# Third buffer for both split feed-forward weights, with their loads and splits written one group earlier (adaLN + S4D + ReLU feed-forward, one core)

## The chip, the cores and the metric

One core of one Trainium2 chip. The metric is the device time of one launch in microseconds (us). The kernel before takes 1416.15 us, the median of 3 runs (1416.11 to 1416.56).

## What is computed

One transformer-like block over 2048 tokens of width 576, in float32: a modulation from `c`, a layer norm, an S4D long convolution with a skip, a gated residual, a second layer norm, a ReLU feed-forward of 576 -> 4608 -> 576, and a second gated residual.

```python
mod = (_silu(c) @ w_mod).reshape(c.shape[0], 6, 1, -1)
sa, ca, ga, sb, cb, gb = (mod[:, i] for i in range(6))
h = _layernorm(x) * (1 + ca) + sa
x = x + ga * _A_ref(h, ...)      # S4D: K = 2 Re(C P); y = irfft(rfft(u) * rfft(K)); y + u * D_skip
h = _layernorm(x) * (1 + cb) + sb
x = x + gb * _B_ref(h, w1, w2)   # max(h @ w1, 0) @ w2, w1 576 x 4608, w2 4608 x 576
```

## The kernel before

Every large matmul is done in three products: each operand is split into a high part (type fp32r) and a low part, the rest, and high x high, high x low and low x high are added up in PSUM.

**Stages.** The tokens are taken in 4 blocks of 512. A prologue (to 229 us) makes what the first block needs: the convolution kernel's first part, the convolution of block 0, the second norm, and the normed, transposed activations as `xh`, `xl` and `xs` (high, low, and the packed fifth slice). Then the feed-forward runs in 144 groups, 36 per block; one group takes 128 of the 4608 hidden columns. Beside the groups of a block run generators for the rest: in block 0 the rest of the convolution kernel (VectorE rotations into `W1r`, TensorE products `kps`) and the convolution of block 1; in block 1 the output of block 0 and the convolution of block 2; in block 2 the output of block 1 and the convolution of block 3; in block 3 the output of block 2. `step()` draws from them at a rate per block; it is called four times per group, within `first` and `second` and behind each.

**One group.** `load_r1(g)` (L1230) and `load_r2(g)` (L1234) bring the raw weights: `r1`, 320 KB, 128 hidden columns of the first matrix, and `r2`, 288 KB, as many rows of the second; both are issued by SyncE (SP) into tiles with two buffers. `split1(g)` makes `w1`: ScalarE (ACT) copies the high part (L1246) and VectorE (DVE) subtracts for the low part (L1249). `split2(g)` does the same for `w2` (ACT L1256, DVE L1259 and L1260). The DVE parts exist in block 0 only: there the low parts are stored to DRAM (`L1d`, `L2d`; the list `late`, L1348, on SP's queue), and from group 36 on they are loaded back instead, `w<-L1d` in `low1` (L1239) and `w<-L2d` in `split2` (L1263), also on SP's queue. `w1` and `w2` tiles have two buffers each. `first(g)` is 14 matmuls (L1273) of `xs`, `xh`, `xl` with `w1` into `hps`; ACT makes `hh` = relu (L1278) and DVE `hl`, its low part (L1279). `second(g)` is 14 matmuls (L1299) of `hh`, `hl` with `w2` into five accumulators `acc`.

**Order.** What is written through `Kept` keeps the order of the program on its engine, and shows with the line L47 in the profile. Everything else is put in order, engine by engine, by a scheduler, so the order written in `ffn` is its input and not its outcome. In the loop, group g writes: the load of `r1` two groups ahead and of `r2` one group ahead, the stores that are due, `split2(g)`, `split1(g+1)`, `first(g)`, `low1(g+2)`, a step, `second(g-1)`. Every engine runs its own list in order, so an instruction that waits holds back all behind it; SP's list holds the loads of `r1`, `r2`, both low parts and the stores.

**Names in the convolution.** `Z` are evacuated transforms, `K`, `U`, `Ua` spectra of kernel and input, `T` and `Y` the complex products (DVE, L994 to L1000), `V` and `W` what the inverse transform `ps_i` (TensorE, L1021) reads, `x` the residual stream that DVE updates from `ps_i`. `Ua` is loaded back from DRAM (`Ud`) by GpSimd (POOL).

Of the kernel before, what the change touches and what calls it, by code (L numbers as in the profile page):

```python
# [11 lines left out]
F32R = mybir.dt.float32r  # L12
# [6 lines left out]
P = 128  # L19
# [30 lines left out]
class KGen:  # L50
# [10 lines left out]
    def v(self, out, a, b, op):  # L61
        self.tc.keep_in_program_order(self.nc.vector.tensor_tensor(out, a, b, op=op))
# [471 lines left out]
class Body:  # L534
# [198 lines left out]
    def main(self, ctx, kg, hooks):  # L733
# [31 lines left out]
        with ExitStack() as c:  # L765
            self.cps = self.pool(c, "cps0", space=PSUM)
            self.tps = self.pool(c, "tps", space=PSUM)
            self.cv = self.pool(c, "cv0", side="right")
            self.cvl = self.pool(c, "cvl", side="right")
            self.nps = 4  # L770
            mods, ffn = self.mod_late(), self.ffn(gens)
            self.vec = Kept(tc, nc.vector)
            for w in self.conv(0):
                if w == "mod":
                    next(mods, None)
                elif w in ("weights", "split"):
                    next(ffn)
                elif w == "rows":
                    hooks[w]()
                elif w in hooks:  # L780
                    for _ in hooks[w]:
                        pass
            self.vec = nc.vector
# [437 lines left out]
    def ffn(self, gens):  # L1221

        nc, I, ff = self.nc, self.I, self.ff
        n = NB * NF
        r1, r2, w1, w2 = {}, {}, {}, {}
        late = []

        def load_r1(g):
            r1[g] = ff.tile([P, 5, P], F32, tag="r1", bufs=2, name="r1")
            nc.sync.dma_start(out=r1[g], in_=I["w1"][g % NF])  # L1230

        def load_r2(g):
            r2[g] = ff.tile([P, D], F32, tag="r2", bufs=2, name="r2")
            nc.sync.dma_start(out=r2[g], in_=I["w2"][(g % NF) * P : (g % NF) * P + P, :])  # L1234

        def low1(g):
            w = w1[g] = ff.tile([P, 2, 5, P], F32R, tag="w1", bufs=2, name="w1")
            if g >= NF:
                nc.sync.dma_start(  # L1239
                    out=w[:, 1].rearrange("p k c -> p (k c)").bitcast(F32), in_=self.L1d[g % NF]  # L1240
                )

        def split1(g):

            w, r = w1[g], r1.pop(g)
            nc.scalar.activation(w[:, 0], r, AF.Copy)  # L1246
            vec = Kept(self.tc, nc.vector) if g < 3 else nc.vector
            if g < NF:
                vec.tensor_tensor(w[:, 1], r, w[:, 0], op=ALU.subtract)  # L1249
                late.append((self.L1d[g], w[:, 1].rearrange("p k c -> p (k c)")))  # L1250

        def split2(g):

            w = w2[g] = ff.tile([P, 1152], F32R, tag="w2", bufs=2, name="w2")
            r = r2.pop(g)
            nc.scalar.activation(w[:, 0:D], r, AF.Copy)  # L1256
            if g < NF:
                v = (Kept(self.tc, nc.vector) if g < 2 else nc.vector).tensor_tensor
                v(w[:, D:640], r[:, 512:D], w[:, 512:D], op=ALU.subtract)  # L1259
                v(w[:, 640:], r[:, :512], w[:, :512], op=ALU.subtract)  # L1260
                late.append((self.L2d[g], w[:, D:]))
            else:
                nc.sync.dma_start(out=w[:, D:].bitcast(F32), in_=self.L2d[g % NF])  # L1263

        def first(g):
            xh, xl, xs = self.xT[g // NF]
            w = w1.pop(g)
            ps = self.fps.tile([P, 512], F32, tag="hps", bufs=2, name="hps")
            ops = [(w[:, 0, 4], xs), (w[:, 1, 4], xs)]
            for k in range(4):  # L1270
                ops += [(w[:, 0, k], xh[:, k]), (w[:, 0, k], xl[:, k]), (w[:, 1, k], xh[:, k])]
            for i, (a, x) in enumerate(ops):
                nc.tensor.matmul(ps, a, x, start=(i == 0), stop=(i == 13))  # L1273
                if i == 6:
                    step(g)
            hh = ff.tile([P, 512], F32R, tag="hh", bufs=2, name="hh")
            hl = ff.tile([P, 512], F32R, tag="hl", bufs=2, name="hl")
            nc.scalar.activation(hh, ps, AF.Relu)  # L1278
            nc.vector.scalar_tensor_tensor(hl, ps, 0.0, hh, op0=ALU.max, op1=ALU.subtract)  # L1279
            return hh, hl  # L1280

        def second(g, hh, hl):
            f = g % NF
            if f == 0:
                self.acc = [
                    self.fps.tile([P, 512], F32, tag=f"acc{i}", name=f"acc{i}_{g}")
                    for i in range(5)
                ]
            acc, w = self.acc, w2.pop(g)
            tail = [(4, w[:, 512:640], hh), (4, w[:, 512:640], hl)]  # L1290
            ops = []
            for i in range(4):
                tk = slice(i * P, (i + 1) * P)
                ops += [(i, hh[:, tk], w[:, 0:512]), (i, hh[:, tk], w[:, 640:]), (i, hl[:, tk], w[:, 0:512])]
            ops = tail + ops if f == NF - 1 else ops + tail
            seen = [0] * 5
            for j, (i, a, x) in enumerate(ops):
                seen[i] += 1
                nc.tensor.matmul(  # L1299
                    acc[i], a, x,  # L1300
                    start=(f == 0 and seen[i] == 1),
                    stop=(f == NF - 1 and seen[i] == (3 if i < 4 else 2)),
                )
                if j == 6:
                    step(g)

        done, recent = [0.0], []

        def step(g):

            at[0] += 1
            target = self.rate(g // NF) * (at[0] % 144 or 144)
            gen = gens[g // NF]
            v = pe = 0.0
            room = (9.0, 7.0, 7.0, 7.0)[g // NF] - sum(recent[-3:])
            recent.append(0.0)
            while done[0] < target and v < min(room, 2.7) and pe < 2:
                w = next(gen, 0)
                if gen.gi_frame is None or w == -1:
                    return  # L1320
                if w is None:
                    pe += 1
                    done[0] += 0.7
                else:
                    v += w
                    recent[-1] = v
                    done[0] += w

        at = [0]
        load_r1(0)  # L1330
        load_r1(1)
        load_r2(0)
        yield
        low1(0)
        low1(1)
        split1(0)
        split2(0)
        split1(1)
        yield
        prev = None  # L1340
        for g in range(n + 1):
            if g < n:
                if g + 2 < n:
                    load_r1(g + 2)
                if g + 1 < n:
                    load_r2(g + 1)
                for dst, src in late:
                    nc.sync.dma_start(out=dst, in_=src.bitcast(F32))  # L1348
                late.clear()
                if g:  # L1350
                    split2(g)
                    if g + 1 < n:
                        split1(g + 1)
                new = (g, *first(g))
                if g + 2 < n:
                    low1(g + 2)
                step(g)
            if prev is not None:
                second(*prev)
                if prev[0] % NF == NF - 1:  # L1360
                    self.evacuate(prev[0] // NF)
            if g < n:
                prev = new
                step(g)
                if g % NF == NF - 1:
                    for _ in gens[g // NF]:
                        pass
                    done[0] = 0.0
# [126 lines left out]
```

## Time and profile before

| what | value |
|---|---|
| median of 3 runs | 1416.15 us |
| the profiled execution's own device time | 1418.65 us |
| its span on the core | 1416.8 us |
| TensorE (PE) busy | 1263.9 us (89%), 10720 matmuls |
| VectorE (DVE) busy | 891.7 us (63%) |
| ScalarE (ACT) busy | 495.4 us (35%) |
| GpSimd (POOL) busy | 180.1 us (13%) |
| DMA | 348.21 MB, mean 246 GB/s |

The mean granted TensorE clock of that execution is 0.938. By stage, each row a stretch of the span:

| stretch, us | what runs | PE busy, us | DVE busy, us | DMA share |
|---|---|---|---|---|
| 0 to 229 | prologue | 140.76 | 189.00 | 0.70 |
| 229 to 300 | feed-forward of block 0, kernel rotations | 65.75 | 64.03 | 0.71 |
| 300 to 400 | the same | 94.24 | 77.93 | 0.72 |
| 400 to 500 | the same, transforms of block 1 | 91.86 | 66.66 | 0.77 |
| 500 to 570 | end of block 0 | 57.51 | 51.37 | 0.71 |
| 570 to 700 | last of block 0, start of block 1 | 112.82 | 102.73 | 0.71 |
| 700 to 800 | block 1 | 100.00 | 50.88 | 0.76 |
| 800 to 890 | end of block 1 | 83.92 | 76.94 | 0.85 |
| 890 to 1000 | into block 2 | 110.00 | 54.75 | 0.65 |
| 1000 to 1100 | block 2 | 98.06 | 93.75 | 0.91 |
| 1100 to 1407 | end of block 2, block 3 | 307.00 | 58.77 | 0.63 |

How to read it: busy shares say little by themselves. A stretch in which PE is busy throughout can only be shortened by fewer matmuls or a higher clock; in the others, what ended PE's idle time (the releaser, written `<-` behind a row) says what set the pace.

### The profile page before, as it was taken

What the parts mean: (1) busy time and instruction counts of PE and PEld (TensorE: products, weight loads), DVE (VectorE), ACT (ScalarE), POOL (GpSimd) and SP (SyncE); (2) the same over time, 40 slices, a digit from 0 to 9 for tenths busy, and PEclk for the clock granted to TensorE, in tenths of its full rate; (3) what the DMA queues carried; (4) which work ended last, traced back from release to release, by engine and by line L of the source; (5) the groups of instructions that cost most, each with busy time, mean ns of one, the idle gap of its engine ahead of it and who ended that gap; (6) DMA issues with size and microseconds to landing.
All of it is one profiled execution on the core that took longest, in us unless ns stands there. A gap on an engine that the chain in (4) does not pass through costs nothing.

```text
span 1416.8 us, 26161 instructions
## 1 busy us (share of the span) xinstructions
PE 1263.9 (89%) x10720; PEld 996.0 (70%) x10720; DVE 891.7 (63%) x1324; ACT 495.4 (35%) x863; POOL 180.1 (13%) x277
## 2 busy tenths in 40 slices
PE   4665687999988987788999998999999999999997
PEld 2444555777867765566777786777887878888886
DVE  5899967999574776958835779463889432101102
ACT  4688323122221431161224322633322253323321
POOL 0667521000110100011010110010000000000000
PEclk9577777999999998899999999999999999999999
DMA  8658865867696767569777988585989657666662
GB/s 255 246 193 313 315 224 181 288 214 256 239 374 228 256 223 280 167 253 346 282 243 252 339 295 293 159 282 152 375 294 350 201 153 228 194 201 195 195 198 98
DMA packets 120845, 348.21 MB, mean 246 GB/s; under 512 B 23949, under 2 KB 24245, under 8 KB 109717
## 3 DMA queue, kind: packets, MB, share of 16 engines
q1 hardware_dynamic: 102260, 222.09, 47.9%
q0 software_dynamic: 17952, 123.08, 22.9%
q8 instruction: 84, 1.38, 0.4%
q10 hardware_dynamic: 512, 1.38, 0.3%
q14 instruction: 37, 0.30, 0.1%
HBM read 262.73 MB, written 83.76 MB: 245 GB/s over the span
## 4 chain that ended last, share of the span: by engine, by line
PE 66%; DVE 8%; DMA 7%; issue 2%; ACT 1%; POOL 0%; SPq 0%; POOLq 0%; ACTq 0%; DVEq 0%
PE hps L1273 28%; PE acc L1299 28%; PE kps L490 4%; PE ps_f L815 3%; DMA w<-L2d 2%; DMA L1d<-w 2%; DMA w<-L1d 2%; PE ps_i L1021 1%; DVE T L459 1%; DVE Y L1000 1%; DVE W1r L461 1%; DMA Ud<-U 1%; DVE T L998 1%; DVE W1r L465 0%; DVE w L1249 0%
## 5 line engine op out<-in xcount | busy, mean ns | idle before, releaser
L1273 PE MATMUL hps<-xh,w 128*128 128x512 f32 x1152 | 396.4, 404 | 0.0
L1299 PE MATMUL acc<-w,hh 128*128 128x512 f32 x1152 | 370.5, 403 | 6.6 <-DMA w<-L2d 6.2
L1279 DVE SCALAR_TENSOR_TENSOR hl<-hps,hh 128x512 fp32r<-128x512 f32 x144 | 99.1, 688 | 326.5 <-ACT hh L1278 326.2
L1299 PEld LDWEIGHTS acc<-w,hh 128*128 128x128 f32 x1152 | 217.3, 190 | 56.8 <-DMA w<-L2d 7.5
L1273 PEld LDWEIGHTS hps<-xh,w 128*128 128x128 f32 x1152 | 220.7, 192 | 48.6 <-ACT xh L1116 0.2
L1299 PE MATMUL acc<-w,hl 128*128 128x512 f32 x576 | 228.3, 409 | 13.2 <-DVE hl L1279 13.2
L1273 PE MATMUL hps<-xl,w 128*128 128x512 f32 x576 | 235.1, 408 | 1.6 <-DVE xl L47 1.6
L1278 ACT ACTIVATE hh<-hps 128x512 fp32r<-128x512 f32 x144 | 86.0, 597 | 366.0 <-PE hps L1273 364.2
L1256 ACT ACTIVATE w<-r 128x576 fp32r<-128x576 f32 x144 | 98.8, 686 | 251.4 <-issue 175.4
L1299 PEld LDWEIGHTS acc<-w,hl 128*128 128x128 f32 x576 | 109.7, 191 | 37.5 <-DVE hl L1279 14.1
L1273 PEld LDWEIGHTS hps<-xl,w 128*128 128x128 f32 x576 | 110.9, 193 | 26.6 <-DVE xl L47 2.7
L1273 PE MATMUL hps<-xs,w 128*128 128x512 f32 x288 | 101.7, 422 | 17.8 <-DMA w<-L1d 7.2
L1246 ACT ACTIVATE w<-r 128x640 fp32r<-128x640 f32 x144 | 105.4, 732 | 34.6 <-DMA L1d<-w 34.5
L490 PEld LDWEIGHTS kps<-W1r,W2r 128*32 128x32 f32 x3456 | 68.1, 146 | 39.8 <-issue 28.2
L490 PE MATMUL kps<-W1r,W2r 128*32 128x48 f32 (+2 forms) x3456 | 78.3, 238 | 14.9 <-issue 11.5
L71 PE MATMUL kps<-W,W 128*32 128x16 f32 x2304 | 45.1, 218 | 44.2 <-POOL W L68 29.0
L71 PEld LDWEIGHTS kps<-W,W 128*32 128x32 f32 x2304 | 40.5, 150 | 55.7 <-POOL W L68 31.4
L1000 DVE TENSOR_TENSOR Y<-Y,T 128x1152 f32<-128x1152 f32 x60 | 79.4, 1350 | 0.0
L1273 PEld LDWEIGHTS hps<-xs,w 128*128 128x128 f32 x288 | 55.0, 194 | 33.4 <-DMA w<-L1d 8.9
L816 ACT ACTIVATE Z<-ps_f 128x288 f32<-128x288 f32 x120 | 48.8, 408 | 68.8 <-PE ps_f L815 67.6
L1409 POOL DMA_DIRECT2D out_dram<-x x16 | 8.7, 546 | 462.8 <-DVE x L1401 460.4
L1299 PE MATMUL acc<-hh,w 128*128 128x512 f32 x144 | 57.4, 398 | 2.5 <-DVE w L1259 1.3
(234 smaller groups left out, 1590.1 us busy)
## 6 DMA issues: line engine op xcount, KB each, us to landing
r<-in_w_dram SPq DMA_DIRECT2D x144, 320.0 KB
r<-in_w_dram SPq DMA_DIRECT2D x144, 288.0 KB, 3.2
w<-L1d SPq DMA_DIRECT2D x108, 320.0 KB, 3.7
w<-L2d SPq DMA_DIRECT2D x108, 288.0 KB
W2r<-W2d POOLq DMA_DIRECT2D x18, 1536.0 KB, 8.8
W2d<-W SPq DMA_DIRECT2D x12, 1536.0 KB, 8.6
Ua<-Ud POOLq DMA_DIRECT2D x15, 1152.0 KB, 10.2
W<-W1d POOLq DMA_DIRECT2D x18, 768.0 KB, 9.4
```

Source lines behind the costliest of these rows:

```text
L71: self.tc.keep_in_program_order(self.nc.tensor.matmul(*args, **kw))
L459: v(T.rearrange(flat), X.rearrange(flat), zi, op=ALU.mult)
L490: nc.tensor.matmul(ps[32 * dd : 32 * dd + 32, q, :], W2[:, r, :, ch], W1[:, :, r, ch], start=(r == 0), stop=(r == 1),)
L815: nc.tensor.matmul(o, fc[:, n2, c, :], src(n2), start=True, stop=True)
L816: ev = nc.scalar.activation(Z[:, n2, c], ps[:, :PC], AF.Copy)
L1000: v(y, y, T, op=op or ALU.add)
L1246: nc.scalar.activation(w[:, 0], r, AF.Copy)
L1256: nc.scalar.activation(w[:, 0:D], r, AF.Copy)
L1273: nc.tensor.matmul(ps, a, x, start=(i == 0), stop=(i == 13))
L1278: nc.scalar.activation(hh, ps, AF.Relu)
L1279: nc.vector.scalar_tensor_tensor(hl, ps, 0.0, hh, op0=ALU.max, op1=ALU.subtract)
L1299: nc.tensor.matmul(acc[i], a, x, start=(f == 0 and seen[i] == 1), stop=(f == NF - 1 and seen[i] == (3 if i < 4 else 2)),)
```

## The change

`w1` and `w2` get a third buffer; `r1` and `r2` keep two. In the loop the loads of the raw weights are written one group earlier (`r1` three groups ahead, `r2` two), `split2` works for group g+1 and `split1` for group g+2 and both stand behind `first(g)`, and `low1` (with the reload of the low part) works for group g+3. Ahead of the loop two more raw loads are issued and a third `w1` tile is asked for. The DVE part of a split keeps its program order (`Kept`) for groups 0 and 1 of `w1` (before: 0 to 2) and for group 0 of `w2` (before: 0 and 1).

```diff
         def low1(g):
-            w = w1[g] = ff.tile([P, 2, 5, P], F32R, tag="w1", bufs=2, name="w1")
+            w = w1[g] = ff.tile([P, 2, 5, P], F32R, tag="w1", bufs=3, name="w1")
...
-            vec = Kept(self.tc, nc.vector) if g < 3 else nc.vector
+            vec = Kept(self.tc, nc.vector) if g < 2 else nc.vector
...
-            w = w2[g] = ff.tile([P, 1152], F32R, tag="w2", bufs=2, name="w2")
+            w = w2[g] = ff.tile([P, 1152], F32R, tag="w2", bufs=3, name="w2")
...
-                v = (Kept(self.tc, nc.vector) if g < 2 else nc.vector).tensor_tensor
+                v = (Kept(self.tc, nc.vector) if g < 1 else nc.vector).tensor_tensor
...
-        low1(0)
-        low1(1)
+        for g in range(3):
+            low1(g)
         split1(0)
         split2(0)
         split1(1)
         yield
+        load_r2(1)
+        load_r1(2)
         prev = None
         for g in range(n + 1):
             if g < n:
+                if g + 3 < n:
+                    load_r1(g + 3)
                 if g + 2 < n:
-                    load_r1(g + 2)
-                if g + 1 < n:
-                    load_r2(g + 1)
+                    load_r2(g + 2)
                 for dst, src in late:
                     nc.sync.dma_start(out=dst, in_=src.bitcast(F32))
                 late.clear()
-                if g:
-                    split2(g)
-                    if g + 1 < n:
-                        split1(g + 1)
                 new = (g, *first(g))
+                if g + 1 < n:
+                    split2(g + 1)
                 if g + 2 < n:
-                    low1(g + 2)
+                    split1(g + 2)
+                if g + 3 < n:
+                    low1(g + 3)
                 step(g)
```

What it moves on the engines. First, DVE in the prologue, at the first complex product of the convolution of block 0 and the second product that follows it; `w_2977` is `w2` of group 1 and `w_3018` that of group 2, `r_2938` and `r_2944` their raw weights.

```order
 L47 TENSOR_TENSOR Y_0_2710<-Y_0_2710,T 128x4x288
 L47 TENSOR_TENSOR T<-K_0_2659,U_0_2633 128x1152
+L1259 TENSOR_TENSOR w_2977<-r_2938,w_2977 128x64
 L47 TENSOR_TENSOR Y_0_2710<-Y_0_2710,T 128x4x288
+L1260 TENSOR_TENSOR w_2977<-r_2938,w_2977 128x512
 L47 TENSOR_TENSOR V_0_2719<-Y_0_2710 128x576 x4
 L47 TENSOR_TENSOR K_1_2724<-Z 128x576 x2
```

The low part of `w2` of group 1 has moved from behind the start of the feed-forward to a place between the last two steps of that product, and the low part of group 2 stands in the second product in the same way.

Second, DVE in the second norm of block 0, and ACT at the same place; `w_2839` is `w1` of group 2, `r_2940` its raw weights.

```order
 L47 TENSOR_TENSOR x_0_280<-ps_i,x_0_280 128x4x72
 L47 BN_STATS st_2819<-x_0_280 128x6 x2
+L1249 TENSOR_TENSOR w_2839<-r_2940,w_2839 128x640
 L47 BN_AGGR mv_288<-st_2819 128x2
 L47 RECIPROCAL mv_288<-mv_288 128x1
```

```order
 L857 ACTIVATE Z<-ps_f 128x288 x3
+L1256 ACTIVATE w_3018<-r_2944 128x576
 L714 ACTIVATE row_gb<-mps_gb 128x128
 L716 ACTIVATE row_gb<-mps_gb 32x64 x2
+L1246 ACTIVATE w_2839<-r_2940 128x640
 L47 ACTIVATE mv_288<-mv_288,eps 128x1 x2
```

Both halves of that split now stand inside the norm, ACT's copy ahead of the square root `mv` and DVE's subtraction ahead of the aggregation; they stood behind the start of the feed-forward.

Third, PE behind `second(0)` at the start of the feed-forward, before (`w_2972` is `w1` of group 2 there, `w_2985` is `w2` of group 1, `w_3011` `w1` of group 3):

```order
L1299 MATMUL acc_0_3017<-hl,w_2841 128x512
L1273 MATMUL hps<-xs_2816,w_2972 128x512
L1299 MATMUL acc_0_3013<-w_2985,hh 128x512
L1299 MATMUL acc_0_3014<-w_2985,hh 128x512
L1299 MATMUL acc_0_3015<-w_2985,hh 128x512
L1299 MATMUL acc_0_3016<-w_2985,hh 128x512
L1273 MATMUL hps<-xs_2816,w_3011 128x512
L1299 MATMUL acc_0_3017<-hh,w_2985 128x512
```

and now (`w_2839` is `w1` of group 2, `w_2977` is `w2` of group 1):

```order
L1299 MATMUL acc_0_3030<-hl,w_2842 128x512
L1273 MATMUL hps<-xs_2816,w_2839 128x512 x2
L1273 MATMUL hps<-xh_2814,w_2839 128x512
L1273 MATMUL hps<-xl_2815,w_2839 128x512
L1273 MATMUL hps<-xh_2814,w_2839 128x512 x2
L1273 MATMUL hps<-xl_2815,w_2839 128x512
```

Single matmuls of `first` and `second` of different groups alternated there, each waiting for its part; now all of `first(2)` stands ahead of `second(1)`.

## The prediction

> **What bounds the kernel now.** I read the chain of waits first, its shares by engine and by line.
>
> ```profile
> PE 66%; DVE 8%; DMA 7%; issue 2%; ACT 1%; POOL 0%; SPq 0%; POOLq 0%; ACTq 0%; DVEq 0%
> PE hps L1273 28%; PE acc L1299 28%; PE kps L490 4%; PE ps_f L815 3%; DMA w<-L2d 2%; DMA L1d<-w 2%; DMA w<-L1d 2%; PE ps_i L1021 1%; DVE T L459 1%; DVE Y L1000 1%; DVE W1r L461 1%; DMA Ud<-U 1%; DVE T L998 1%; DVE W1r L465 0%; DVE w L1249 0%
> ```
>
> Two thirds are matmuls, which the change leaves alone. But 2% each go to the reloads of the low parts (`w<-L1d`, `w<-L2d`) and the stores (`L1d<-w`): the transfers around the two tiles that get a third buffer. In order of time, the longest such pieces (start, duration) are:
>
> ```profile
> 295.27 11.28 DMA L1d<-w
> ...
> 554.10 15.81 DMA L1d<-w
> 629.00 17.10 DMA w<-L2d
> 800.19 10.13 DMA w<-L1d
> 846.38 15.61 DMA w<-L2d
> 1056.04 12.60 DMA w<-L1d
> ```
>
> The groups by line say what engines lost to them (last column: idle time before, and its releasers).
>
> ```profile
> L1299 PE MATMUL acc<-w,hh 128*128 128x512 f32 x1152 | 370.5, 403 | 6.6 <-DMA w<-L2d 6.2 <-ACT hh L1278 0.2
> L1299 PE MATMUL acc<-w,hl 128*128 128x512 f32 x576 | 228.3, 409 | 13.2 <-DVE hl L1279 13.2
> L1273 PE MATMUL hps<-xs,w 128*128 128x512 f32 x288 | 101.7, 422 | 17.8 <-DMA w<-L1d 7.2 <-ACT w L1246 3.9 <-DVE hl L1279 2.3
> L1246 ACT ACTIVATE w<-r 128x640 fp32r<-128x640 f32 x144 | 105.4, 732 | 34.6 <-DMA L1d<-w 34.5
> ```
>
> PE waited 7.2 + 6.2 = 13.4 us for reloads, 3.9 for a copy. ACT waited 34.5 us before its copies into `w1`, because the store that reads the tile's previous contents had not landed: a wait for a buffer. Single rows of PE's timeline place the waits:
>
> ```profile
> 248.26 0.47 PE L1273 MATMUL hps<-xs,w 128*128 128x512 f32 x1 [2.30 <-DVE hl L1279]
> 249.97 0.50 PE L1299 MATMUL acc<-hh,w 128*128 128x512 f32 x1 [1.24 <-DVE w L47]
> ...
> 308.34 1.29 PE L490 MATMUL kps<-W1r,W2r 128*32 128x48 f32 x48 [3.25 <-ACT ker L500]
> ...
> 565.38 0.80 PE L1273 MATMUL hps<-xs,w 128*128 128x512 f32 x1 [3.90 <-ACT w L1246]
> ...
> 588.23 2.07 PE L1299 MATMUL acc<-w,hl 128*128 128x512 f32 x4 [8.04 <-DVE hl L1279]
> ...
> 639.78 0.80 PE L1273 MATMUL hps<-xs,w 128*128 128x512 f32 x1 [2.76 <-DMA w<-L1d]
> ...
> 862.03 0.80 PE L1299 MATMUL acc<-w,hh 128*128 128x512 f32 x1 [3.59 <-DMA w<-L2d]
> ...
> 1068.68 0.50 PE L1273 MATMUL hps<-xs,w 128*128 128x512 f32 x1 [1.94 <-DMA w<-L1d]
> ```
>
> Each wait also cost clock. The rows by stretch (length, busy time of PE, weight loads, DVE, ACT, POOL, then the granted clock, the DMA share and GB/s):
>
> ```profile
> 248.00:254.00 6.00, 4.50 (x12) 3.19 (x13) 6.00 (x8) 0.00 (x0) 1.06 (x2) 0.72 0.69 264
> 862.00:868.00 6.00, 5.97 (x14) 4.72 (x15) 6.00 (x6) 0.00 (x0) 0.00 (x0) 0.50 0.91 359
> 1068.00:1074.00 6.00, 5.32 (x16) 4.22 (x17) 5.94 (x6) 0.44 (x1) 0.00 (x0) 0.72 1.05 428
> 1250.00:1300.00 50.00, 50.00 (x222) 41.42 (x221) 5.53 (x8) 14.78 (x24) 0.00 (x0) 1.00 0.69 199
> 250.00:300.00 50.00, 49.87 (x541) 38.62 (x542) 50.00 (x53) 11.25 (x19) 4.79 (x9) 0.97 0.75 255
> 300.00:350.00 50.00, 46.75 (x604) 36.51 (x606) 47.94 (x52) 11.19 (x20) 2.12 (x4) 0.97 0.70 249
> 700.00:800.00 100.00, 100.00 (x816) 77.47 (x815) 50.88 (x78) 35.52 (x74) 10.99 (x17) 1.00 0.76 263
> ```
>
> At full clock a matmul takes 50/222 = 0.225 us, a group of 28 6.3 us (1250 to 1300: PE is the bound, nothing to gain). Behind 862 the clock was 0.50: 14 matmuls took 6.0 us instead of 3.15, so that wait cost 3.59 + 2.85.
>
> **The change part by part.** *Prologue: a loss that is nearly sure.* Not kept in order any more, three DVE splits slid ahead of the feed-forward. DVE and ACT there:
>
> ```profile
> 180.40 1.36 DVE L47 TENSOR_TENSOR Y<-Y,T 128x1152 f32<-128x1152 f32 x1
> 181.79 3.23 DVE L47 TENSOR_TENSOR V<-Y 128x576 f32<-128x576 f32 x4
> ...
> 195.74 0.67 ACT L1256 ACTIVATE w<-r 128x576 fp32r<-128x576 f32 x1
> ...
> 197.82 2.90 DVE L47 TENSOR_TENSOR K<-Z 128x576 f32<-128x576 f32 x6 [12.80 <-ACT Z L857]
> 215.44 2.29 DVE L47 TENSOR_TENSOR w<-r,w 128x640 fp32r<-128x640 f32 x4
> ...
> 228.94 0.70 PE L1273 MATMUL hps<-xs,w 128*128 128x512 f32 x2 [2.14 <-DVE xs L47]
> ```
>
> The split of `w2(1)` now stands ahead of the `Y` at 180.40 and waits for ACT's copy, which ends at 195.74 + 0.67 = 196.41 and keeps its place on ACT. Behind the waiting instruction are `Y` and `V`: 196.41 + split 0.75 + `Y` 1.36 + `V` 3.23 = 201.75 until `K` starts, against 197.82: +3.9. (A split is costed from the row at 215.44: 2.29 us for two of `w1` and the two rows of one of `w2`, so 0.75 each.) `w2(2)`, in the next product, adds 0.75, `w1(2)`, in the norm, 0.75: **+5.4**. Behind 197.82 DVE has no gap to absorb it, and PE's first feed-forward matmul waits for DVE (2.14, `xs`). Lower bound 5.2, if the small rows overlap; upper 6.2, if the `r1` of group 2, whose buffer is free only behind the splits at 215.44, lands late: ACT's copy of it now stands ahead of the norm's square root.
>
> *Start of the feed-forward.* Those splits are done, and `first(2)` no longer interleaves with `second(1)`. The 2.30 and 1.24 go. In 248 to 254, 12 matmuls need 2.7 us and took 6.0, 3.3 lost, and 2.0 of the 2.30 lie ahead of that window: **-5.3**. But DVE is the next limit: busy 50.00 of 50 us in 250 to 300. It starts 5.4 later and has 2.25 less to do, so it runs 3.2 behind until 300. Its 2.1 us of idleness in 300 to 350, with PE's 3.25 wait at 308.34 (an ACT queue held by the store of 295.27, for a buffer that the third one supplies), takes that back. Net of prologue and start: **0**, between -2 and +3.
>
> *End of block 0.* Here the convolution's chain runs through DVE:
>
> ```profile
> 565.36 0.82 DVE L1249 TENSOR_TENSOR w<-r,w 128x640 fp32r<-128x640 f32 x1 [11.06 <-ACT w L1246]
> 566.47 2.62 DVE L998 TENSOR_TENSOR T<-K,Ua 128x1152 f32<-128x1152 f32 x2
> ...
> 546.88 0.53 POOL L802 DMA_DIRECT2D Ua<-Ud  x1
> ...
> Ua<-Ud POOLq DMA_DIRECT2D x15, 1152.0 KB, 10.2
> r<-in_w_dram SPq DMA_DIRECT2D x144, 288.0 KB, 3.2
> ```
>
> DVE stood 11.06 us behind ACT, ACT behind the store of 554.10. With a third buffer the copy needs a store one group older, so this wait goes. The product behind it needs `Ua`, asked for at 546.88 and landing 10.2 later, 557.1: at most 566.47 - 557.1 = 9.4 are won. The order has the convolution of block 1 about half a group to a group later against the groups (3 to 6 us), so I take **-4**; bounds -11 (the whole wait) and +4 (the raw load, still two buffers deep, is late in the same burst and holds DVE instead).
>
> *Block 1.* A reload gets one more group of time, 6.3 us. The longest took 17.1, 15.6 and 10.1 us and were late by 4 us at most (3.59), so all 13.4 - 1.94 = 11.5 us of waits of this block are covered, with the clock behind them: 2.85 at 862 and about 1 at 639, 15.3 in all. What limits the gain is the convolution of block 2:
>
> ```profile
> 847.16 1.36 DVE L998 TENSOR_TENSOR T<-K,Ua 128x1152 f32<-128x1152 f32 x1 [6.23 <-DMA Ua<-Ud]
> ...
> 889.33 0.46 DVE L1026 TENSOR_TENSOR x<-ps_i,x 128x288 f32<-128x288 f32 x1 [3.25 <-PE ps_i L1021]
> ```
>
> From 847 to 889 DVE hardly waits for PE, and block 2 starts behind DVE's norm. The waits near 640 (about 6 us with clock) come before that and are won. Of those near 860, 3.25 to 5 are won, the slack that DVE itself lost to PE. **-10**, between -4 (little but the first) and -15.3.
>
> *Block 2 and 3.* The 1.94 at 1068.68 and, in the window behind it, 6.0 - 16 x 0.225 = 2.4 us: **-4** (0 to -4.3). Block 3 is PE's own: 0.
>
> The page TensorE: Matmul & The Clock Gate (section HAM oscillation — how this bites in real kernels) of the Trainium skill has the clock fall after idle gaps above about 3.4 us. The row at 1068.68 idled 1.94 us only and was granted 0.72, so the row decides; by the rule this term would be -2 and the sum 2 us less.
>
> **Sum:** 0 - 4 - 10 - 4 = -18. The profiled execution took 1418.65 us (span 1416.8, 1.85 around it), 2.5 above the median 1416.15; it would take 1400.6, the median **1398 us**. Single terms at their bounds, not all at once, make 1388 to 1410.
>
> **The rivals.**
>
> (a) *The convolution's chain takes over.* DVE's and the DMA's work at the block ends, not the reloads, sets when the next block starts. For it: the 6.23 wait for `Ua`. Against: in 700 to 800 PE was busy 100 of 100 us, DVE 50.88. Then only 3.25 of block 1 and 2 of block 2 are won: 1416 - 5 = **1411**.
>
> (b) *More goes than I count.* The whole 9.4 at block 0's end, the 8.04 at 588.23 behind the same DVE stall, all 15.3 of block 1 and 4: 36.8, so **1380**. Against: the convolution is later in the order.
>
> (c) *DVE held by its own earlier splits: slower.* In block 0 each split stands a group earlier in DVE's list, while its raw load has no more buffers than before. Where a burst on the DMA rings makes that load late, the split holds DVE, `hl` behind it, and PE. It decides once load and copy take longer than a group's 6.3 us; the price is another wait of the size seen at 588.23, 8.04, and the end of block 0 and all later gains gone to the chain in (a): 1416 + 8 = **1424**. For it: what the prologue does is this very thing (12.80 us of idleness turned into work that waits). Against: the middle landing time of an `r2` load is 3.2 us, half a group.
>
> (d) *The change does not do what it says.* The reloads sit in SP's one list, between `r` loads that wait for two buffers, so asking a group earlier may start nothing earlier; and in 1068 to 1074 the rings moved 428 GB/s, more than twice the 199 of a quiet stretch, so a reload in a burst may be limited by what else moves. Then 5.4 stays, without the gains: **1421**. The Trainium skill, page DMA: Bandwidth & Descriptors (section Where 436 GB/s comes from), lets HBM to SBUF transfers bind at about 358 GB/s; the 428 here is above that. By that rule the bursts are full and this case's time is the result.
>
> **How the numbers follow.** Chances: forecast 0.48, (a) 0.14, (b) 0.08, (c) 0.18, (d) 0.12. The range, 1384 to 1424, leaves out (b) and the upper half of (c), 0.17. Where cases of both signs count, the forecast's own range is 1388 to 1410. What can be told from no change is 0.2%, 2.8 us: faster below 1413.3, slower above 1419.0. Faster: 0.48 + 0.08 + 0.09 of (a) = 0.65. Same: 0.05 of (a) and 0.03 of (d) = 0.08. Slower: 0.18 + 0.09 of (d) = 0.27.
>
> **What would show it.** The first feed-forward matmul at 234 instead of 228.94, with DVE idle until 196.4 ahead of `Y`. No `w<-L1d` or `w<-L2d` among PE's releasers; ACT's 34.5 us behind `L1d<-w` near 0; DVE's 11.06 gone. Block 1 shorter by about 10. Wrong would make it: an `hl` wait of PE larger than 13.2 in all (c), reloads still named as releasers (d), or their waits gone with the start of block 2 where it was, a longer wait for `Ua` or `V` in their place (a).

## The result, and the profile after

The changed kernel takes 1403.87 us (median of 6 runs, 1397.55 to 1406.71) against 1416.13 us of the kernel before (6 runs): ratio 0.991, 95% interval 0.9886 to 0.9935. That is 12.3 us less, where 18 were forecast. A second set of runs, beside later experiments, gave 0.994 (0.9917 to 0.9962); one of its six executions ran at a granted clock of 0.73, took 1609.55 us and is not in that ratio.

The chain of waits of the changed kernel, by engine and by line:

```profile
PE 62%; DVE 20%; DMA 9%; issue 4%; ACT 2%; POOL 1%; SPq 0%; ACTq 0%; POOLq 0%; DVEq 0%
PE acc L1299 24%; PE hps L1273 24%; PE kps L490 5%; PE ps_f L815 4%; DMA r<-in_w_dram 3%; DMA Ua<-Ud 3%; DVE T L998 3%; DVE Y L1000 3%; PE kps L71 2%; PE ph L71 2%; DMA Ud<-U 1%; DMA Zr<-Zd 1%; DVE hl L1279 1%; DVE Y L994 1%; DVE T L62 1%
```

The reloads `w<-L1d`, `w<-L2d` and the stores `L1d<-w`, 2% each before, are gone from it. In their place stand the raw loads (`r<-in_w_dram`) and the convolution's products. The groups of instructions, with the idle time before them in the last column:

```profile
L1299 PE MATMUL acc<-w,hh 128*128 128x512 f32 x1152 | 368.2, 402 | 2.8 <-ACT hh L1278 2.8
L1299 PE MATMUL acc<-w,hl 128*128 128x512 f32 x576 | 227.3, 406 | 20.4 <-DVE hl L1279 20.3
L1246 ACT ACTIVATE w<-r 128x640 fp32r<-128x640 f32 x144 | 105.4, 732 | 44.6 <-DMA r<-in_w_dram 44.2 <-DMA w<-L1d 0.4
L1273 PE MATMUL hps<-xs,w 128*128 128x512 f32 x288 | 100.9, 421 | 2.0 <-DVE xs L47 1.8 <-DVE xs L1119 0.3
```

PE's 13.4 us for reloads and 3.9 for a copy are 0. But its waits for `hl` rose from 13.2 to 20.3 in the second row (15.5 to 20.3 over all of PE's rows, since before the first matmuls of a group waited 2.3 more), and ACT, which had waited 34.5 us for stores, now waits 44.2 us for raw loads: a wait changed its name and became no shorter.

Where the time went is read from when groups start: the first matmul (L1273) of group 0, 24, 36 (block 1) and 72 (block 2), in the profiled execution of each kernel. The columns are the us between them.

| kernel | to group 0 | 0 to 24 | 24 to 36 | block 1 | blocks 2, 3 | span |
|---|---|---|---|---|---|---|
| before | 228.9 | 239.0 | 142.4 | 302.8 | 503.7 | 1416.8 |
| the change | 229.1 | 234.8 | 142.8 | 295.1 | 501.4 | 1403.2 |
| the change, second time (e11) | 233.8 | 233.8 | 143.6 | 294.5 | 500.0 | 1405.7 |
| the change without the slide into the prologue (e1) | 228.2 | 236.9 | 142.7 | 294.6 | 499.9 | 1402.3 |
| w1's part of the change (e2) | 228.4 | 234.5 | 140.5 | 297.8 | 502.3 | 1403.5 |
| w2's part of the change (e3) | 231.7 | 236.9 | 142.8 | 301.9 | 499.8 | 1413.1 |
| third buffers alone (e4) | 228.4 | 237.9 | 140.2 | 292.3 | 502.0 | 1400.8 |
| third buffers alone, second time (e12) | 227.5 | 237.7 | 141.2 | 293.8 | 499.9 | 1400.1 |
| w1's buffer alone (e5) | 226.9 | 236.6 | 142.5 | 298.9 | 499.9 | 1404.8 |
| w1's low part alone (e6) | 228.2 | 238.1 | 138.1 | 297.7 | 505.5 | 1407.7 |
| raw buffers alone (e7) | 229.3 | 237.8 | 142.9 | 303.5 | 501.7 | 1415.2 |
| w1's buffer and the raw ones (e8) | 224.9 | 238.4 | 142.0 | 298.2 | 499.9 | 1403.3 |
| w2's buffer alone (e9) | 227.9 | 235.7 | 139.6 | 301.7 | 499.9 | 1404.8 |
| w1's low part, w2 and r1 (e10) | 228.3 | 237.3 | 138.9 | 292.7 | 501.7 | 1399.0 |

Each row is one execution; the two pairs of the same kernel show that a stretch repeats within 1 to 2 us (1.0 up to group 36, 1.5 in block 1, 2.1 behind it), the prologue within 5 only.

### The profile page after: what moved, and what is told of

Same layout as the page of the kernel before. It is cut to its first block, busy times and chain, and to the rows that moved or that the text cites. A ratio compares the mean times of both kernels' runs of the same rounds, so it can differ in the third digit from the quotient of the medians.

```text
span 1403.2 us, 26027 instructions
## 1 busy us (share of the span) xinstructions
PE 1258.5 (90%) x10720; PEld 994.5 (71%) x10720; DVE 889.9 (63%) x1324; ACT 497.4 (35%) x863; POOL 179.2 (13%) x277
## 4 chain that ended last, share of the span: by engine, by line
PE 62%; DVE 20%; DMA 9%; issue 4%; ACT 2%; POOL 1%; SPq 0%; ACTq 0%; POOLq 0%; DVEq 0%
PE acc L1299 24%; PE hps L1273 24%; PE kps L490 5%; PE ps_f L815 4%; DMA r<-in_w_dram 3%; DMA Ua<-Ud 3%; DVE T L998 3%; DVE Y L1000 3%; PE kps L71 2%; PE ph L71 2%; DMA Ud<-U 1%; DMA Zr<-Zd 1%; DVE hl L1279 1%; DVE Y L994 1%; DVE T L62 1%
## 5 line engine op out<-in xcount | busy, mean ns | idle before, releaser
L1273 PE MATMUL hps<-xh,w 128*128 128x512 f32 x1152 | 395.9, 403 | 0.7 <-issue 0.7
L1273 PEld LDWEIGHTS hps<-xh,w 128*128 128x128 f32 x1152 | 219.0, 191 | 47.3
L1299 PE MATMUL acc<-w,hl 128*128 128x512 f32 x576 | 227.3, 406 | 20.4 <-DVE hl L1279 20.3
L1273 PE MATMUL hps<-xl,w 128*128 128x512 f32 x576 | 230.5, 401 | 0.9 <-DVE xl L47 0.9
L1273 PEld LDWEIGHTS hps<-xl,w 128*128 128x128 f32 x576 | 110.0, 191 | 26.9 <-DVE xl L47 2.3
L1246 ACT ACTIVATE w<-r 128x640 fp32r<-128x640 f32 x144 | 105.4, 732 | 44.6 <-DMA r<-in_w_dram 44.2
L1273 PE MATMUL hps<-xs,w 128*128 128x512 f32 x288 | 100.9, 421 | 2.0 <-DVE xs L47 1.8
L1273 PEld LDWEIGHTS hps<-xs,w 128*128 128x128 f32 x288 | 55.7, 196 | 15.1 <-ACT xh L47 2.1
```

Of the source, the lines that this page charges most:

```text
L1299: nc.tensor.matmul(acc[i], a, x, start=(f == 0 and seen[i] == 1), stop=(f == NF - 1 and seen[i] == (3 if i < 4 else 2)),)
```

## The experiments

All ratios are against the kernel before, run beside each experiment, with their 95% intervals. Its median was 1413.71 beside e1 to e4, 1416.7 beside e5 to e8 and 1416.95 beside e9 to e12, so it is the ratios that compare. A ratio lies near the quotient of the means, not of the medians, so it can differ from what two medians give (e9's do by 0.2%).

| run | what it is | median, us | ratio | interval |
|---|---|---|---|---|
| e1_keep3 | the change without the slide into the prologue | 1403.5 | 0.9917 | 0.9895 to 0.9939 |
| e2_w1only | w1's part of the change | 1404.25 | 0.9925 | 0.9907 to 0.9942 |
| e3_w2only | w2's part of the change | 1413.23 | 0.9991 | 0.9974 to 1.0007 |
| e4_bufs_only | both third buffers, nothing moved | 1402.62 | 0.9919 | 0.9903 to 0.9936 |
| e5_w1buf | w1's third buffer, nothing moved | 1408.6 | 0.9953 | 0.9933 to 0.9974 |
| e6_lo3 | the third buffer for w1's low part only | 1408.96 | 0.9946 | 0.9926 to 0.9966 |
| e7_raw3 | third buffers for r1, r2 instead | 1416.4 | 0.9999 | 0.9979 to 1.002 |
| e8_w1buf_r3 | third buffers for w1, r1, r2 | 1408.84 | 0.9952 | 0.9931 to 0.9972 |
| e9_w2buf | w2's third buffer, nothing moved | 1405.59 | 0.9944 | 0.9921 to 0.9968 |
| e10_lo3_w2_r1 | w1's low part, w2 and r1 | 1400.74 | 0.9894 | 0.9874 to 0.9914 |
| e11_after_again | the change, beside e12 | 1407.78 | 0.994 | 0.9917 to 0.9962 |
| e12_bufs_again | e4, beside e11 | 1402.51 | 0.9908 | 0.9887 to 0.9929 |

**e1_keep3**, the changed kernel with the splits of the first groups kept behind the start of the feed-forward.

```diff
-            vec = Kept(self.tc, nc.vector) if g < 2 else nc.vector
+            vec = Kept(self.tc, nc.vector) if g < 3 else nc.vector
...
-                v = (Kept(self.tc, nc.vector) if g < 1 else nc.vector).tensor_tensor
+                v = (Kept(self.tc, nc.vector) if g < 3 else nc.vector).tensor_tensor
```

> The changed kernel with one thing put back: the DVE part of the splits keeps its program order for groups 0 to 2 of w1 and w2, so none of them stands in the prologue any more. My theory: the slide into the prologue costs about 5 us, which the first profile of the change hid because its prologue happened to run 2.4 to 5 us ahead of the one of before from 150 us on. Then DVE no longer waits for ACT's copy ahead of the last Y of the first product, the first feed-forward matmul comes 4 to 5 us earlier counted from that product, and some of it is given back by the three splits (2.25 us of DVE) that return to the start of the feed-forward: 1399 to 1403 us against 1403.9 of the change. Rival: the slide is free or a gain, because the start of the feed-forward is DVE's and it got 2.25 us less to do: 1404 to 1409, with PE's waits of 2.30 for hl and 1.24 for w back near the second group.

1403.5 us, between the two expectations and no different from the change. The slide does cost time in the prologue. The clean measure is the stretch from ACT's last `Z` to the first feed-forward matmul, since what runs ahead of it varies by some us between executions. ACT's rows at the last `Z`, then DVE's row with the moved split and PE's first matmul, in the second execution of the change (e11):

```profile
195.43 0.68 ACT L1256 ACTIVATE w<-r 128x576 fp32r<-128x576 f32 x1
...
198.03 0.41 ACT L857 ACTIVATE Z<-ps_f 128x288 f32<-128x288 f32 x1 [0.56 <-PE ps_f L856]
...
196.14 0.23 DVE L1259 TENSOR_TENSOR w<-r,w 128x64 fp32r<-128x64 f32 x1 [13.62 <-ACT w L1256]
...
233.83 1.19 PE L1273 MATMUL hps<-xs,w 128*128 128x512 f32 x2 [1.76 <-DVE xs L47]
```

and the same in the kernel with the buffers alone (e12):

```profile
196.72 0.41 ACT L857 ACTIVATE Z<-ps_f 128x288 f32<-128x288 f32 x1 [0.56 <-PE ps_f L856]
...
196.19 2.90 DVE L47 TENSOR_TENSOR K<-Z 128x576 f32<-128x576 f32 x6 [12.79 <-ACT Z L857]
...
227.54 1.19 PE L1273 MATMUL hps<-xs,w 128*128 128x512 f32 x2 [1.79 <-DVE xs L47]
```

233.83 - 198.03 = 35.8 us with the slide, 227.54 - 196.72 = 30.8 without; e1 has 31.3, the change's first execution 35.7. DVE idles about as long in both, 13.6 and 12.8 us, but with the slide the last `Y` and `V`, which had been done ahead of the idle time, come behind it, and the other two splits follow. Yet from group 0 to 24 e1 takes 236.9 us, the change 234.8 and 233.8: behind the prologue, where DVE is the bound, the splits save 2 to 3 of the 4.4 us or so that they cost in it.

**e2_w1only** and **e3_w2only**, the change for one matrix alone, buffers and moves; the other is as before. For w1:

```diff
+                if g + 3 < n:
+                    load_r1(g + 3)
...
                 if g:
                     split2(g)
-                    if g + 1 < n:
-                        split1(g + 1)
                 new = (g, *first(g))
                 if g + 2 < n:
-                    low1(g + 2)
+                    split1(g + 2)
+                if g + 3 < n:
+                    low1(g + 3)
```

> The part of the change that concerns w1 alone (third buffer, earlier r1 load, split and reload); w2 and r2 as before. My theory: the waits behind the tile w1 go (7.2 us of PE for w<-L1d, 3.9 for ACT's copy, ACT's 34.5 behind the stores), those for w<-L2d (6.2) stay: two thirds of the gain, 1406 to 1410 us. Rival: PE only waits for w2 instead where it waited for w1, because both sit in one SP list, and little is won: 1412 to 1417.

1404.25: better than my theory. PE's waits for `w<-L2d` stay, 5.42 and 2.45 us long, and still nearly all of the gain is there. For w2 the same was done with `load_r2(g + 2)` and `split2(g + 1)` behind `first(g)`:

> The part of the change that concerns w2 alone (third buffer, earlier r2 load, split and reload); w1 and r1 as before. My theory: 6.2 us of PE's waits for w<-L2d go, the slide of two w2 splits into the prologue costs 4 to 5, w1's waits (7.2, 3.9, ACT's 34.5) stay: 1412 to 1417 us. Rival: the 3.59 at 862 with its slow clock was the wait that decided, and w2 brings most of the gain: 1405 to 1410.

1413.23, ratio 0.9991: nothing won, as my theory had it, but not for the reason alone that it gave. Its groups:

```profile
L1299 PE MATMUL acc<-w,hl 128*128 128x512 f32 x576 | 226.3, 408 | 19.3 <-DVE hl L1279 19.3
...
L1273 PE MATMUL hps<-xs,w 128*128 128x512 f32 x288 | 102.5, 424 | 20.2 <-DMA w<-L1d 12.4 <-DVE w L1249 4.4 <-DVE xs L47 1.7
```

The wait for `w<-L2d` is gone, that for `w<-L1d` rose from 7.2 to 12.4, that for `hl` from 13.2 to 19.3 (over all of PE's rows from 15.5).

**e4_bufs_only**, the kernel before with two numbers changed.

```diff
-            w = w1[g] = ff.tile([P, 2, 5, P], F32R, tag="w1", bufs=2, name="w1")
+            w = w1[g] = ff.tile([P, 2, 5, P], F32R, tag="w1", bufs=3, name="w1")
...
-            w = w2[g] = ff.tile([P, 1152], F32R, tag="w2", bufs=2, name="w2")
+            w = w2[g] = ff.tile([P, 1152], F32R, tag="w2", bufs=3, name="w2")
```

> The kernel before with the third buffer for w1 and w2 and nothing else: loads, splits and reloads are written where they were. If the buffers alone bring the gain (ACT's copies no longer wait for the stores), 1403 to 1409 us and ACT's 34.5 us behind L1d stores near 0. If the earlier asking is needed for it, the reload waits of 13.4 us on PE stay and only the store waits go: 1410 to 1415.

1402.62, just under the first expectation (1403 to 1409): the buffers alone bring the whole gain. Its groups:

```profile
L1299 PE MATMUL acc<-w,hl 128*128 128x512 f32 x576 | 230.3, 411 | 12.8 <-DVE hl L1279 12.8
L1246 ACT ACTIVATE w<-r 128x640 fp32r<-128x640 f32 x144 | 105.5, 733 | 57.6 <-DMA r<-in_w_dram 57.4
L1273 PE MATMUL hps<-xs,w 128*128 128x512 f32 x288 | 99.4, 417 | 6.5 <-DVE hl L1279 4.7 <-DVE xs L47 1.8
```

No reload is among PE's releasers, though their writing was not moved. In the trace, a reload `w<-L1d` is issued 12.8 us ahead of the first matmul (L1273) of its group before, 21.2 here and 21.2 in the change (medians of block 1); `w<-L2d`, which `second` needs about a group later, goes from 0.2 us behind that matmul to 8.5 ahead of it here, and 8.5 in the change. With a tile free a group earlier the reload starts earlier by itself, and as much earlier as with the moved order. The waits for `hl` are 12.8 + 4.7 = 17.5 us here, between the 15.5 before and the 20.3 of the change.

**e5_w1buf** is the first of these two numbers alone, **e9_w2buf** the second alone.

> The kernel before with one number changed: the tile w1 gets a third buffer; w2 keeps two, nothing is written in another place. My theory, formed from the runs so far: the whole gain is ACT's copies into w1 no longer waiting for the L1d stores (34.5 us) and the w1 reloads starting a group earlier: 1402 to 1406 us, as with w1 alone and its order moved. Rival: with both buffers but the old order the time was 1402.6, with w1 and the new order 1404.3; if w2's buffer carries a part, this one stays at 1407 to 1411.

> The kernel before with a third buffer for w2 alone, nothing written elsewhere. With w1's buffer alone the ratio was 0.9953, with both 0.9919. If the two add up, w2's alone is worth 0.3 to 0.4%: 1410 to 1413 us beside 1416. My theory is that they do not: reloads of w1 and w2 sit in one SP list, and PE waits for whichever comes last, so w2's buffer alone only hands the wait to w<-L1d: within 0.2% of the kernel before, with PE's waits for w<-L2d gone and those for w<-L1d above 7.2 us.

1408.6 and 1405.59, ratios 0.9953 and 0.9944. Of e5 its rival held: one buffer is half of it. For e9 both expectations fell, and 1405.59 is better than either: w2's buffer alone is worth 0.56%, and the two add up within the intervals (0.47 + 0.56 = 1.03% against 0.81 and 0.92 measured for both). PE's waits were handed on as expected:

```profile
L1299 PE MATMUL acc<-w,hl 128*128 128x512 f32 x576 | 227.7, 406 | 4.6 <-DVE hl L1279 4.6
L1246 ACT ACTIVATE w<-r 128x640 fp32r<-128x640 f32 x144 | 105.4, 732 | 25.3 <-DMA L1d<-w 24.0 <-DMA r<-in_w_dram 1.3
L1273 PE MATMUL hps<-xs,w 128*128 128x512 f32 x288 | 101.8, 422 | 26.4 <-DMA w<-L1d 10.2 <-DVE w L1249 9.8 <-DVE hl L1279 2.8
```

`w<-L1d` rose from 7.2 to 10.2, and block 1 is only 1.1 us shorter (302.8 to 301.7). Half of the gain of this execution came from block 0, which I had not asked: 239.0 + 142.4 = 381.4 us before, 235.7 + 139.6 = 375.3 here, 6.1 of 12.0. The wait for `hl` fell from 13.2 to 4.6 and ACT's for stores from 34.5 to 24.0. That a copy of w2, waiting in ACT's list for its tile, had held the copies behind it would fit; no run isolates it. Beside e3, this also prices the moved order for w2, its slide into the prologue included: the same buffer with it is 0.9991, without it 0.9944, the intervals (just) apart.

**e6_lo3**: w1 in two tiles, and the third buffer for the low part, which alone is stored and reloaded.

```diff
-            w = w1[g] = ff.tile([P, 2, 5, P], F32R, tag="w1", bufs=2, name="w1")
+            w = ff.tile([P, 5, P], F32R, tag="w1", bufs=2, name="w1")
+            v = ff.tile([P, 5, P], F32R, tag="w1l", bufs=3, name="w1l")
+            w1[g] = (w, v)
```

> The kernel before with w1 as two tiles: the high part with two buffers, the low part, which alone is stored and reloaded, with three. The store reads the low part only, so ACT's copy does not wait for it. My theory: this is the part of the buffer that matters, 1402 to 1407 us. Rival: the high part needs its third buffer too, since ACT's copy then waits for the 14 matmuls that read the tile two groups before: 1409 to 1416.

1408.96, ratio 0.9946, like e5 (0.9953): the time fell between the two expectations, but half the memory does what the whole third buffer of w1 does.

**e7_raw3** and **e8_w1buf_r3**: third buffers for the raw weights, loaded one group earlier, without and with w1's.

```diff
-            r1[g] = ff.tile([P, 5, P], F32, tag="r1", bufs=2, name="r1")
+            r1[g] = ff.tile([P, 5, P], F32, tag="r1", bufs=3, name="r1")
...
-            r2[g] = ff.tile([P, D], F32, tag="r2", bufs=2, name="r2")
+            r2[g] = ff.tile([P, D], F32, tag="r2", bufs=3, name="r2")
...
-                if g + 2 < n:
-                    load_r1(g + 2)
-                if g + 1 < n:
-                    load_r2(g + 1)
+                if g + 3 < n:
+                    load_r1(g + 3)
+                if g + 2 < n:
+                    load_r2(g + 2)
```

> The kernel before with a third buffer for the raw weights r1 and r2 and their loads written one group earlier, w1 and w2 with two as before. In the changed kernel ACT's wait before its copies was not gone but renamed, 44 us for the raw loads. If the raw loads were the wait all along, this wins what the change won: 1403 to 1408 us. If the stores that hold the w1 tile decide (my theory), ACT's 34.5 us behind L1d stores stay and the time stays near 1412 to 1417.

> Third buffers for w1, r1 and r2, raw loads one group earlier, w2 with two. If the wait for the raw loads, which now holds ACT for 44 to 57 us, still costs time, removing it wins more than the change: 1393 to 1400 us, with fewer hl waits of PE at the end of block 0. If the convolution's chain through DVE and Ua already sets the end of block 0, it costs nothing: 1400 to 1405, ACT's wait gone and nothing else moved.

1416.4 and 1408.84: by themselves the raw buffers win nothing (0.9999), as my theory had it, and on top of w1's nothing (0.9952 against 0.9953), where both expectations for e8 had been lower (1393 to 1400, 1400 to 1405). In e8 ACT's copies into w1 no longer wait for raw loads, but for stores again, 19.8 us in all. At the end of block 0 ACT's copy waited for such a store and DVE behind it, with three buffers for w1:

```profile
558.94 0.74 ACT L1246 ACTIVATE w<-r 128x640 fp32r<-128x640 f32 x1 [10.56 <-DMA L1d<-w]
...
560.29 0.23 DVE L1259 TENSOR_TENSOR w<-r,w 128x64 fp32r<-128x64 f32 x1 [6.41 <-ACT w L1256]
...
565.19 0.83 DVE L1249 TENSOR_TENSOR w<-r,w 128x640 fp32r<-128x640 f32 x1 [2.74 <-ACT w L1246]
```

**e10_lo3_w2_r1** takes e6 with `bufs=3` for w2 and r1 and `load_r1(g + 3)`.

> All that stood in the way by turns, within the memory there is: w1 in two tiles with three buffers for the low part alone, three for w2 and three for r1, whose load is written one group earlier. It tells what holds DVE at the end of block 0, where the change won at the first product with Ua and lost it again 8 us later to a raw load. If it is the buffers, each uncovered in turn, then DVE's waits for ACT between 550 and 570 are gone and the time is 1396 to 1400 us. If the convolution's own chain sets the end of block 0 (my present theory, since neither a third raw buffer nor w1's own moved it), the waits go elsewhere again and it is 1401 to 1405, as with the two buffers alone.

1400.74, between the two expectations; ratio 0.9894, the fastest here, though not told apart from the buffers alone (0.9919, 0.9908). The stall stood there once more, 8.68 us, now behind the copy of w2, whose raw tile `r2` has two buffers in this run, while the DMA share was 1.01. DVE's rows, ACT's copy and the stretch from 555 to 560 us (busy time of PE, weight loads, DVE, ACT, POOL, then clock, DMA share, GB/s):

```profile
549.63 2.63 DVE L998 TENSOR_TENSOR T<-K,Ua 128x1152 f32<-128x1152 f32 x2 [0.35 <-DMA Ua<-Ud]
...
561.67 0.23 DVE L1261 TENSOR_TENSOR w<-r,w 128x64 fp32r<-128x64 f32 x1 [8.68 <-ACT w L1258]
...
560.95 0.68 ACT L1258 ACTIVATE w<-r 128x576 fp32r<-128x576 f32 x1 [13.50 <-DMA r<-in_w_dram]
...
555.00:560.00 5.00, 2.55 (x12) 1.77 (x10) 0.00 (x0) 0.00 (x0) 0.00 (x0) 1.00 1.01 416
```

**e11_after_again** and **e12_bufs_again** are the change and e4 once more, side by side.

> The changed kernel itself, once more, beside the next run on the same chip, to tell whether the moved order has a price or a gain of its own over the buffers alone. If the slide of three splits into the prologue costs the median what it costs in the prologue (about 4 us from the last Z to the first feed-forward matmul), it is 3 to 4 us slower than the next one; if the start of the feed-forward takes it back (my theory), within 2 us of it: 1401 to 1405 us.

> The kernel before with the two third buffers and nothing moved, once more, beside the changed kernel on the same chip. My theory: 1401 to 1405 us, within 2 us of the changed kernel. Rival: 3 to 4 us faster than it, having no prologue slide.

1407.78 and 1402.51, ratios 0.994 and 0.9908. Side by side the change is 5.3 us slower, so the theory of both expectations (within 2 us, 1401 to 1405) did not hold for the change, and the rival (3 to 4 us slower) came nearer. The first pair, which did not run side by side, had been 0.991 and 0.9919, the other way round. The means of the two, 0.9925 and 0.9914, are 0.1% apart, less than the intervals resolve. The moved order has no gain of its own. That it has a price for both matrices together is likely: in the table of stretches the two executions of the change take 2.5 us more than the two of the buffers alone from group 24 to 36, and 1.8 more in block 1. It is not shown clear of the noise.

## Why the prediction was right, and where it was not

**Prologue and start, forecast 0: right in both parts.** The slide was forecast at +5.4 and is 35.8 - 30.8 = 5.0 here, 4.4 against the mean of e1, e4 and e12 (31.3). In the second execution the first matmul came at 233.83, forecast 234; in the first the part ahead of it ran 5 us early (the last `Z` at 193.37 against 198.34 before), so its 229.1 shows nothing of it. From group 0 to 24 the two executions won 4.2 and 5.2, which takes the slide back: from the last `Z` to group 24 it is 269.6 us before, 270.6 and 269.6 in the change.

**End of block 0, forecast -4: this step failed.** From group 24 to 36 the change took 0.4 and 1.2 us more than before. DVE's rows there:

```profile
554.43 0.23 DVE L1259 TENSOR_TENSOR w<-r,w 128x64 fp32r<-128x64 f32 x1 [2.83 <-ACT w L1256]
...
557.11 0.82 DVE L1249 TENSOR_TENSOR w<-r,w 128x640 fp32r<-128x640 f32 x1 [1.85 <-ACT w L1246]
...
558.22 2.62 DVE L998 TENSOR_TENSOR T<-K,Ua 128x1152 f32<-128x1152 f32 x2
...
566.52 0.82 DVE L1249 TENSOR_TENSOR w<-r,w 128x640 fp32r<-128x640 f32 x1 [5.08 <-ACT w L1246]
...
568.00 2.62 DVE L994 TENSOR_TENSOR Y<-K,Ua 128x1152 f32<-128x1152 f32 x2
```

The first product came 8.25 us earlier, at 558.22 instead of 566.47. Of these, 4.0 had been won ahead of group 24 (463.93 instead of 467.90), so 4.3 here, about the 4 that was forecast. Then DVE stopped for the next split, whose raw load had been asked for at 550.79 and took 14.85 us:

```profile
550.79 14.85 DMA r<-in_w_dram
```

2.83 + 1.85 + 5.08 = 9.8 us of idleness for 11.1 before. The prediction had this as the bound of +4 (the raw load holds DVE instead) and weighed it too low. In e8 and e10 the stall was handed on again, to a store and to the raw load of w2. What does not change is the traffic: POOL asks for five transfers for the convolution between 543.5 and 549.7 us (546.4 and 552.5 before), and from 555 to 560 the rings moved 406 GB/s before, 417 in the change, at a share of 1.00. The store asked for at 554.10 before took 15.81 us, the raw load in the change 14.85. The stretch before, then in the change:

```profile
555.00:560.00 5.00, 5.00 (x24) 4.11 (x23) 0.00 (x0) 0.00 (x0) 0.00 (x0) 1.00 1.00 406
...
555.00:560.00 5.00, 5.00 (x24) 4.13 (x23) 3.15 (x5) 1.23 (x2) 0.00 (x0) 1.00 1.00 417
```

So what rival (d) says of a reload in a burst, that bandwidth limits it, fits the transfers at this place. Its other half, that asking earlier starts nothing earlier, fell: the reloads start 8 us earlier (e4 above). That bandwidth is the cause here is not shown: fewer or later bytes there were not tried, and no run had three buffers for r1, r2, w1 and w2 at once.

Nor is the stall all of this stretch. With the same buffers and the old order it is shorter: 140.2 and 141.2 us with both third buffers (the change 142.8 and 143.6), 139.6 with w2's alone (142.8 with its order moved, e3), and 138.9 in e10, 3.5 us less than before. So gains of the size of the forecast were to be had here; all four executions with the moved order of w2 lack them (142.7 to 143.6). By which wait it takes them back was not followed up.

**Block 1, forecast -10: -7.7 and -8.3.** All waits for reloads went, as forecast. The size was too large by a fifth; new waits for `hl` came here (1.79 and 2.38 us in the first execution, with the clock behind the second). With the buffers alone, which have one such wait above 1 us here, it is -10.5 and -9.0. The convolution does not take the gain away: rival (a) left only 3.25 for this block, so it fell here.

**Blocks 2 and 3, forecast -4: -2.4 and -3.7.** The 1.94 us wait and the slow stretch behind it are gone. That the third buffer did this is not shown: the wait is also absent where w1 has two buffers (e3, e7, e9, with 499.8, 501.7 and 499.9 us for these blocks), and the stretch repeats within 2 us only.

**Rival (c)** was named as a `hl` wait above 13.2. That figure is one row's; over all of PE's rows the waits are 15.5 us before, 20.3 and 22.7 in the change and 24.4 in e1, against 17.5 and 18.5 with the buffers alone and 7.4 with w2's. So its sign came, at 2 to 5 us more for the change than for the buffers alone, where it was priced at 8, and the reloads won more. Its mechanism, a split that waits and holds `hl` behind it, is at most a part of it. The longest of these waits, 6.09 us, has DVE busy with the convolution's products ahead of `hl`, and no split:

```profile
528.30 2.63 DVE L1000 TENSOR_TENSOR Y<-Y,T 128x1152 f32<-128x1152 f32 x2
530.83 0.69 DVE L1279 SCALAR_TENSOR_TENSOR hl<-hps,hh 128x512 fp32r<-128x512 f32 x1
...
531.58 1.65 PE L1299 MATMUL acc<-w,hl 128*128 128x512 f32 x3 [6.09 <-DVE hl L1279]
```

The next longest, 5.48 us at 573.81, does come behind the split that waited 5.08 us above, but the buffers alone have one of 5.46 near it (at 584.47).

**The sum, forecast -18.** By span the two executions are 13.6 and 11.1 us shorter, but 5.0 of the 13.6 are the prologue that happened to run early. Counted from the last `Z`, it is -8.7 and -10.8: about 5 us of the difference to the forecast are the end of block 0, about 2 block 1, up to 2 blocks 2 and 3. The direction and the mechanism (reloads that PE no longer waits for) were right; the median's 12.3 us in the first set of runs are nearer to 18 than these sums, and the 0.6% of the second set, some 8.5 us, agree with them.

**What the prediction did not see:** the moved order was taken as the means by which the loads come earlier. It is not. The third buffers alone reach 0.9919 and 0.9908 with two numbers changed, and ask for the reloads as early.

## What to carry to other kernels

When a wait on a buffer is to be removed, try the buffer first and alone: where loads are issued as soon as a tile is free, they move up without being written earlier, and work moved up for them can stand in the way on an engine that runs its list in order (5 us in this prologue). Look at which transfers are under way during a stall before buying a buffer against it: here, at a DMA share of 1.00, three sets of buffers changed the stall's releaser and left 8.7 to 9.8 of its 11.1 us. Buffer only the part of a tile that the slow transfer touches; here half of w1 did as much as the whole (0.9946 and 0.9953).

## What the runs showed of the hardware

Some short gaps of PE cost clock, and others of like length do not. The stretches of 4 us that begin at a matmul which had waited 2.83, 2.38 and 1.79 us in the changed kernel (PE at 280.6, 858.3 and 632.6):

```profile
280.60:284.60 4.00, 4.00 (x98) 3.13 (x99) 4.00 (x6) 0.49 (x2) 0.00 (x0) 0.50 0.70 255
...
858.30:862.30 4.00, 4.00 (x12) 3.20 (x13) 4.00 (x4) 1.51 (x3) 0.00 (x0) 0.66 1.04 403
632.60:636.60 4.00, 3.99 (x17) 3.30 (x18) 3.97 (x4) 0.69 (x1) 0.18 (x1) 1.00 1.03 426
```

The granted clock was 0.50 and 0.66 behind the first two and 1.00 behind the third. The Trainium skill, page TensorE: Matmul & The Clock Gate (section HAM oscillation — how this bites in real kernels), puts the limit at gaps above about 3.4 us; here 2.4 us were enough. But the length alone does not decide, and that each wait cost clock, as the prediction has it, is too strong: in the kernel before, matmuls that had waited 2.65 us (at 405.20) and 2.04 us (at 854.96) were followed by 4 us at full clock, the 1.94 us at 1068.68 by 6 us at 0.72.

```profile
405.20:409.20 4.00, 4.00 (x34) 3.34 (x34) 1.40 (x2) 0.52 (x2) 1.58 (x3) 1.00 0.70 205
855.00:859.00 4.00, 3.44 (x14) 2.51 (x14) 2.62 (x3) 0.74 (x2) 0.00 (x0) 1.00 1.02 426
```

Whether shorter gaps close by add to it was not separated.

Six executions of the changed kernel spread from 1397.55 to 1406.71, 0.65%, and its two profiled executions reached group 0 at 229.1 and 233.8 us. One profile tells little of an edit to the prologue; the stretch from a fixed event just ahead of it tells more: from the last `Z` the same two took 35.7 and 35.8.
